# Two of the first stage's token blocks at 384 columns instead of three at 256

## The chip, the cores and the metric

The kernel runs as one program on one core of one Trainium2 chip. The number that is compared is the device time of one execution in microseconds (us), the median of several. A core has five engines that run their own instruction streams and wait for each other by semaphores: TensorE (PE, matrix products; its weight loads are shown as PEld), VectorE (DVE), ScalarE (ACT), GpSimd (POOL) and SyncE (SP), which here issues the DMAs.

## The reference

q, k and v are [4, 8, 576, 64]: batch, heads, positions, features. All arithmetic is float32.

```python
# attention: two parts, added
q_d, k_d, v_d = (mean over groups of 4 positions)          # 144 positions
out_up = repeat(softmax(q_d k_d^T / 8) v_d, 4 times)       # coarse part
out_local = softmax(where(|i-j| < 4, q k^T / 8, -1e9)) v   # a window of 7 positions
x = (out_up + out_local) as [2304 tokens, 512]
# first stage (called stage 1 here), d_ff = 1536
xn = x / rms(x) * rms_g
g = xn @ w_gate
x = (g * sigmoid(g) * (xn @ w_val)) @ w_out
# second stage (stage 2), d_ff = 2048
x = relu(x @ w_in)**2 @ w_out2
```

## The kernel before

**Numbers.** A float32 product is made of three passes in the faster fp32r format: every operand is split into a high and a low part (tiles `hi`/`lo`, `xh`/`xl`, `hh`/`hl`), and TensorE does high x high, high x low and low x high. The weights come in 64-bit words from DRAM and are split by `decode`: one ACT operation, four or five on VectorE, and an addition, a rounding and a subtraction that go to GpSimd, ACT or VectorE.

**Attention.** The first batch is done by TensorE (`wide`, `wide_post`, six pieces of 96 tokens). The coarse part of all batches is done in 16 pieces (`down`, a batch and a pair of heads each). The local part of the other three batches is done on GpSimd and VectorE in 14 units of mostly 128 tokens (`attend`, `local`): for each of a unit's four rows GpSimd multiplies queries with a window of keys (`pr<-k,q`), VectorE sums (`sc<-pr`), and later GpSimd multiplies the window of values with the weights (`pr<-v,es`) and VectorE sums into `xa`. There are two `xa` buffers (`XAB`). `post` adds the coarse part, computes the root mean square with a small TensorE product (`t<-ss,on`), scales, transposes and writes a block's input tiles `xh` and `xl`. There are two of each, so the tiles of a block take the place of those of the block but one before.

**Stage 1.** The 2304 tokens are nine blocks of 256 (`BLK`). For each block six rounds `fp` go over 256 inner features each: `hidden` does 24 matmuls of the gate into PSUM bank g, tanh on ACT, a VectorE operation (`th<-th,g`), 24 matmuls of the value into bank v, a VectorE product (`v<-v,th`), a rounding (`hh<-v`, ACT or VectorE) and a subtraction (`hl<-v,hh`); `outp` then does 24 matmuls into the block's output sums, in the two banks a (even blocks) or b (odd). A matmul has a 128x128 weight and 256 columns of tokens. `y_out` copies the sums through a tile `vv` to DRAM. All 18 weight tiles of the stage stay in SBUF; those of stage 2 take their places while the last block runs.

**Stage 2.** Four blocks of 512 tokens and one of 256, 16 rounds each of 128 inner features.

**Order.** `PLAN` is a string that sets the order in which work is recorded: d coarse pieces, a and b the first batch, w weights, u units, p posts, x the rounds of stage 1 (`SEQ` gives the order of the first twelve, which belong to two blocks). Buffers are handed out in that order, in rings, so a tile waits for the user of the same buffer that was recorded before it. `Plan.order` then sorts the operations with a model of their times, forward and backward in turn, `ROUNDS` times with a random jitter (`SEED`), and keeps the best. The instructions are issued in that order on every engine; what may run on more than one engine (`VP`, `AV`) is assigned there. `TAGS` names the PSUM banks of the coarse pieces and the first batch, and for each half of a weight tile how it is decoded. Until stage 1 begins, idle time of TensorE is filled with dummy matmuls (line 466, into bank v).

Of the kernel before, what the change touches and what calls it, by code (L numbers as in the profile page):

```python
# [13 lines left out]
F32 = mybir.dt.float32  # L14
# [34 lines left out]
TAGS = ('dbg- dtg- dbg- dgg- bdd- bdd- bdd- bdd- ttd- ttd- ttd- ttd- add- add- add- add- '  # L49
        'aagg aagg aagt bbtd bbdd bbtd bdt tdt gta gdt gdt btt '  # L50
        '-- -- a3 a3 -- -- -- -- -- -- -- -- -- -- -- -- -- -- -- g1 g1 -- -- -- -- -- -- -- -- -- -- -- -- -- -- --')
# [12 lines left out]
SEED = 1  # L64
# [412 lines left out]
def attn_moe_kernel(ctx: ExitStack, tc, qs, kw, vw, qt, kt, vt, v4, wg, wv, wo, w2i, w2o, gw, gb,  # L477
# [7 lines left out]
    seq1 += [(j, fp) for j in range(len(set(SEQ)), len(BLK)) for fp in range(NP1)]  # L485
# [13 lines left out]
    def bank(tag, dtype=F32):  # L499
        return tile("ps", tag, [128, 512], dtype, 2 if tag in "ab" else 1)  # L500
# [5 lines left out]
    g_sb = tile("const", "g", [128, 4])  # L506
    mk_sb = tile("const", "mk", [128, 70])
    xr_sb = tile("const", "xr", [128, 4, 64])
# [34 lines left out]
    def decode(src, n, hi, lo, st, how="--"):  # L543
# [6 lines left out]
        low = lw if how[0] == "-" else bank(how[0], I32)  # L550
        A.activation(low, lw.bitcast(U32), AF.Copy, scale=2.0**-29)
        part = lw if how[1] == "1" else low
        V.scalar_tensor_tensor(out=part, in0=hw, scalar=-0x40000000, in1=low, op0=ALU.bitwise_and,
# [10 lines left out]
        if how[1] == "3":  # L564
            hf = low.bitcast(F32)
        AV.copy(hi[:, cs], hf)
        (V if how[1] == "3" else VP).tensor_tensor(out=lo[:, cs], in0=hf, in1=hi[:, cs].bitcast(F32), op=ALU.subtract)
# [27 lines left out]
    def weights1(fp, m):  # L595
        src = (wg, wv, wo)[m]
        n = fp * 3 + m
        how = TAGS.split()[28 + 2 * n:30 + 2 * n]
        hi, lo = slots(n) if n < 16 else [spare([128, 1024], F32R) for i in range(2)]
        for n in range(2):  # L600
            st = staging() if fp < 5 else tile("stage", "st", [128, 512, 2], I32, 3)
            decode(src[fp], n, hi, lo, st, how[n])
        W1[fp, m] = hi, lo
# [93 lines left out]
    def xtile(j):  # L697
        if j not in xtiles:
            xtiles[j] = [tile("xt", t, [128, 4, BN], F32R, 2) for t in ("xh", "xl")]
        return xtiles[j]  # L700
# [155 lines left out]
    def post(j):  # L856

        xh, xl = xtile(j)
        n0 = 0
        if j == 2:  # L860
            n0 = 64
            AV.copy(xh[:, :, 0:64], xr_sb)
            VP.tensor_tensor(out=xl[:, :, 0:64], in0=xr_sb, in1=xh[:, :, 0:64].bitcast(F32), op=ALU.subtract)
        nt = (BN - n0) // RUNS
        ss = tile("sm", "ss", [128, 8], F32, 2)
        mb = bank("t")
        o = 0
        for u in BLOCKS[j]:
            w = u.cnt
            od = tile("lc", "pr", [128, 2, 128], F32, 2)[:, 0:w // 2]  # L870
            a = 0
            for s in u.segs:
                DQ.dma_start(
                    out=od[:, a:a + s.cnt // 2],
                    in_=od_d[s.b - 1].rearrange("(p u) e -> p u e", u=NU)[:, s.t // 2:(s.t + s.cnt) // 2])
                a += s.cnt // 2
            xv = u.xa.rearrange("p (a w) e -> p a w e", w=2)
            VP.tensor_tensor(out=xv, in0=xv, in1=od.unsqueeze(2).to_broadcast([128, w // 2, 2, 128]), op=ALU.add)
            for i in range(w):
                A.activation(mb[:, 0:128], u.xa[:, i, :], AF.Square, accum_out=ss[:, o + i:o + i + 1])  # L880
            o += w
        mp = mb[:, 128:128 + nt]
        T.matmul(out=mp, lhsT=on_sb, rhs=ss[:, 0:nt], start=True, stop=True)
        ms = tile("sm", "ms", [128, 8], F32, 2)[:, 0:nt]
        V.tensor_scalar(out=ms, in0=mp, scalar1=1.0 / DM, scalar2=1e-6, op0=ALU.mult, op1=ALU.add)
        P.tensor_tensor(out=ms, in0=ms, in1=half_neg[:, 0:nt], op=ALU.pow)
        o = 0
        for u in BLOCKS[j]:
            w = u.cnt
            for i in range(w):  # L890
                A.activation(u.xa[:, i, :], u.xa[:, i, :], AF.Copy, scale=ms[:, o + i:o + i + 1])
            tp = bank("t")
            with plan.joint():
                for i in range(w):
                    T.transpose(tp[:, i * 128:(i + 1) * 128], u.xa[:, i, :], id_sb)
            tv = tp[:, 0:w * 128].rearrange("p (x k c) -> p k x c", k=4, c=RUNS)
            ns = slice(n0 + o * RUNS, n0 + (o + w) * RUNS)
            for k in range(4):
                hv, lv = (t[:, k, ns].rearrange("p (x c) -> p x c", c=RUNS) for t in (xh, xl))
                g = g_sb[:, k:k + 1]  # L900
                A.activation(hv, tv[:, k], AF.Copy, scale=g)
                V.scalar_tensor_tensor(out=lv, in0=tv[:, k], scalar=g, in1=hv.bitcast(F32), op0=ALU.mult,
                                       op1=ALU.subtract)
            o += w

    yps, hid = {}, {}

    def gemm(p, w, xh, xl, c):
        whi, wlo = (t.rearrange("p (k f) -> p k f", k=4) for t in w)
        cs = slice(c * 128, c * 128 + 128)  # L910
        with plan.joint():
            for k in range(4):
                T.matmul(out=p, lhsT=whi[:, k, cs], rhs=xh[:, k, :], start=(c == 0 and k == 0), stop=False,
                         skip_group_check=True)
                T.matmul(out=p, lhsT=whi[:, k, cs], rhs=xl[:, k, :], start=False, stop=False,
                         skip_group_check=True)
# [3 lines left out]
    def hidden(j, fp):  # L920
        xh, xl = xtiles[j]
        n = BLK[j]
        gp = bank("g")[:, 0:2 * n].rearrange("p (c n) -> p c n", c=2)
        for c in range(2):
            gemm(gp[:, c, :], W1[fp, 0], xh, xl, c)
        th = tile("hp", "th", [128, 2, n], F32, 2)
        A.activation(th, gp, AF.Tanh, scale=0.5)
        V.scalar_tensor_tensor(out=th, in0=th, scalar=1.0, in1=gp, op0=ALU.add, op1=ALU.mult)
# [250 lines left out]
```

## Time and profile before

| | |
|---|---|
| median of 3 runs | 1000.95 us (1000.70 to 1002.62) |
| the profiled execution | 1000.25 us, span 998.0 us |
| granted TensorE clock, mean | 0.998 |

```profile
PE 980.2 (98%) x6866; PEld 906.4 (91%) x6866; DVE 587.6 (59%) x985; ACT 417.0 (42%) x984; POOL 442.3 (44%) x298
...
PE   7998999999999999999999999999999999999998
...
DVE  6999899786687857575634568963222322322232
...
POOL 2566688867656676676733465863001000100000
```

The first line is the busy time of each engine with its share of the span and its instructions. The others cut the span into 40 slices of 25 us; a digit is the busy share of a slice in tenths. TensorE is busy nearly all the time after the first slices, VectorE is full in the first quarter and GpSimd has most of its work in the first half.

### The profile page before, as it was taken

Reading aid. Unit: us, or ns where it says so; the run is one execution under the profiler, and the core shown is the slowest. Engines: PE = TensorE matmul, PEld = TensorE weight load, DVE = VectorE, ACT = ScalarE, POOL = GpSimd, SP = SyncE. Lnnn points to the kernel's source line nnn. Section 1 sums busy time; section 2 is a strip of 40 time slices with the busy share of each in tenths; the row PEclk is TensorE's granted clock in tenths of the full one; section 3 lists DMA queues with packets and bytes.
Section 4 is the critical chain, followed back from the end, with each engine's and each line's share of the span. In section 5 each row is a group of like instructions: output and inputs, shape, how many; then the busy total and the mean of one; then the engine's idle time right before and its main releaser. Section 6 shows DMA issues by size and latency. Waiting matters only on the chain.

```text
span 998.0 us, 17246 instructions
## 1 busy us (share of the span) xinstructions
PE 980.2 (98%) x6866; PEld 906.4 (91%) x6866; DVE 587.6 (59%) x985; ACT 417.0 (42%) x984; POOL 442.3 (44%) x298
## 2 busy tenths in 40 slices
PE   7998999999999999999999999999999999999998
PEld 7888999999999999999999998888888888888897
DVE  6999899786687857575634568963222322322232
ACT  5787665532435342323244557663222212322232
POOL 2566688867656676676733465863001000100000
PEclk9999999999999999999999999999999999999999
DMA  9954553253262523222011446334000100100010
GB/s 282 262 160 157 175 179 103 73 151 113 85 182 80 171 78 115 93 65 96 28 33 60 132 128 209 104 109 137 1 1 1 54 0 1 43 1 1 1 43 22
DMA packets 38465, 92.93 MB, mean 93 GB/s; under 512 B 4218, under 2 KB 14498, under 8 KB 38386
## 3 DMA queue, kind: packets, MB, share of 16 engines
q1 hardware_dynamic: 38386, 91.84, 29.6%
q8 instruction: 54, 0.88, 0.4%
q14 instruction: 25, 0.20, 0.1%
HBM read 80.62 MB, written 11.21 MB: 92 GB/s over the span
## 4 chain that ended last, share of the span: by engine, by line
PE 89%; DVE 5%; POOL 2%; DMA 2%; issue 1%; ACT 1%; SPq 0%; DVEq 0%; POOLq 0%; ACTq 0%
PE v L473 25%; PE g L473 24%; PE a L473 20%; PE b L473 15%; DVE b L473 2%; PE d L473 2%; DVE st L473 2%; PE t L473 2%; PE v L466 1%; DMA b<-in_qt 1%; DMA st<-in_wg 1%; POOL w L473 0%; POOL st L473 0%; POOL pr L473 0%; POOL b L473 0%
## 5 line engine op out<-in xcount | busy, mean ns | idle before, releaser
L473 PE MATMUL g<-xh,w 128*128 128x256 f32 (+1 forms) x776 | 176.8, 307 | 0.4 <-DVE th L473 0.4
L473 PE MATMUL v<-xh,w 128*128 128x256 f32 (+1 forms) x632 | 147.6, 311 | 0.5 <-DVE hl L473 0.5
L473 DVE SCALAR_TENSOR_TENSOR v<-v,th 128x512 f32<-128x512 f32 (+1 forms) x94 | 63.3, 674 | 128.6 <-ACT th L473 101.3
L473 PEld LDWEIGHTS g<-xh,w 128*128 128x128 f32 x776 | 131.1, 191 | 7.0 <-ACT xh L473 0.6
L473 ACT ACTIVATE th<-g 128x512 f32<-128x512 f32 (+1 forms) x94 | 54.5, 580 | 198.1 <-PE g L473 194.8
L473 POOL TENSOR_TENSOR pr<-v,es 128x896 f32<-128x896 f32 x54 | 99.4, 1939 | 65.7 <-DVE es L473 28.2
L473 PE MATMUL v<-xh,b 128*128 128x256 f32 (+1 forms) x552 | 123.9, 303 | 0.1
L473 POOL TENSOR_TENSOR pr<-k,q 128x896 f32<-128x896 f32 x54 | 115.4, 2158 | 9.6 <-DVE sc L473 7.2
L473 PE MATMUL g<-xl,w 128*128 128x256 f32 (+1 forms) x388 | 118.3, 305 | 0.1
L473 PEld LDWEIGHTS v<-xh,w 128*128 128x128 f32 x632 | 107.7, 191 | 7.1 <-PE g L473 0.7
L473 POOL TENSOR_TENSOR xl<-st,xh 128x1024 fp32r<-128x1024 f32 (+1 forms) x10 | 21.6, 2179 | 184.7 <-ACT xh L473 184.7
L473 PE MATMUL v<-xl,w 128*128 128x256 f32 (+1 forms) x316 | 97.9, 310 | 0.0
L473 PEld LDWEIGHTS v<-xh,b 128*128 128x128 f32 x552 | 93.0, 191 | 4.4 <-PE g L473 0.3
L473 PE MATMUL g<-xh,b 128*128 128x256 f32 (+1 forms) x408 | 94.4, 310 | 0.2 <-DVE th L473 0.2
L473 ACT CAST hh<-v 128x512 fp32r<-128x512 f32 (+1 forms) x94 | 53.5, 569 | 81.6 <-DVE v L473 71.3
L473 PE MATMUL v<-xl,b 128*128 128x256 f32 (+1 forms) x276 | 83.1, 301 | 0.0
L473 DVE SCALAR_TENSOR_TENSOR g<-g,th 128x512 f32<-128x512 f32 (+1 forms) x40 | 25.8, 645 | 95.5 <-ACT th L473 95.4
L473 DVE TENSOR_TENSOR hl<-v,hh 128x512 fp32r<-128x512 f32 (+1 forms) x94 | 62.4, 664 | 26.3 <-ACT hh L473 24.6
L473 PEld LDWEIGHTS g<-xl,w 128*128 128x128 f32 x388 | 74.1, 191 | 3.6 <-DVE xl L473 0.3
L473 POOL TENSOR_TENSOR st<-st 128x512 int32<-128x512 int32 x48 | 55.9, 1166 | 41.5 <-DVE st L473 39.4
L473 PEld LDWEIGHTS g<-xh,b 128*128 128x128 f32 x408 | 69.1, 190 | 4.2 <-issue 0.3
L473 ACT ACTIVATE st<-st 128x512 int32<-128x512 uint32 (+1 forms) x96 | 64.7, 684 | 18.7 <-DVE st L473 11.2
(207 smaller groups left out, 2336.8 us busy)
## 6 DMA issues: line engine op xcount, KB each, us to landing
k<-in_kw SPq DMA_DIRECT2D x12, 640.0 KB
v<-in_vw SPq DMA_DIRECT2D x12, 640.0 KB
st<-in_w2i SPq DMA_DIRECT2D x14, 512.0 KB
st<-in_w2o SPq DMA_DIRECT2D x14, 512.0 KB
y<-vv SPq DMA_DIRECT2D x18, 256.0 KB
out<-xh SPq DMA_DIRECT2D x18, 256.0 KB
st<-y SPq DMA_DIRECT2D x8, 512.0 KB
st<-in_wg SPq DMA_DIRECT2D x7, 512.0 KB
```

Source lines behind the costliest of these rows:

```text
L466: self.nc.tensor.matmul(out=out, lhsT=one, rhs=one, start=True, stop=True)
L473: getattr(self.hw[on[op]], method)(*args, **kw)
```

## The change

- `BLK` becomes six blocks of 256 and two of 384 tokens. The units of the last three blocks are spread over two: the seventh block takes three units, the eighth three.
- In a block of 384, `hidden` does its work in pieces of 128 inner features: 12 matmuls of 384 columns into g, 12 into v, the same four operations on 128x384 instead of 128x512, and `outp` 12 matmuls. The output sums take four banks (a, a, b, b). `outp` records its work in four groups, one for each output slice, and a slice that is complete is copied out at once.
- `post` works on one unit instead of a block: each unit has its own small product for the root mean square, its own scale and its own transposes.
- `th` has one buffer instead of two, in stage 2 too; `vv` is gone, and `y_out` uses the ring `st` that the weights and the later coarse pieces are staged in (for the last block a tile of the ring `xh`). Its copy may go to ACT or VectorE.
- The special ways to decode four halves of weight tiles are gone: two halves (`a3`) had their additions and subtraction on VectorE with the low part in PSUM bank a, two (`g1`) held the low part in bank g. All halves are now decoded in SBUF.
- `PLAN`, `SLOT`, `TAGS`, `ROUNDS` and `SEED` are others.

```diff
-         5: [[(2, 4, 4)], [(2, 8, 4)]], 6: [[(2, 12, 4)], [(2, 16, 2), (3, 16, 2)]],
-         7: [[(3, 0, 4)], [(3, 4, 4)]], 8: [[(3, 8, 4)], [(3, 12, 4)]]}
-BLK = [256] * 9
+         5: [[(2, 4, 4)], [(2, 8, 4)]], 6: [[(2, 12, 4)], [(2, 16, 2), (3, 16, 2)], [(3, 0, 4)]],
+         7: [[(3, 4, 4)], [(3, 8, 4)], [(3, 12, 4)]]}
+BLK = [256, 256, 256, 256, 256, 256, 384, 384]
...
-PLAN = 'd2 d3 d0 d1 a0 b0 w00 a2 a1 w01 w12 b1 a4 b2 a3 a5 w11 w21 b4 w20 w10 b3 w02 w30 u1 w32 b5 d7 u0 d5 d4 d6 w22 E w31 w41 w40 w50 x x w42 x x d10 x x w52 w51 x x x x x p2 x u2 d11 u3 p3 x d8 x x u5 d9 u4 x x x p4 u6 x x d12 x x x d15 d14 d13 x u7 p5 u8 x u9 x x x x x p6 x x x u10 x x x u11 x x p7 x x u12 u13 x x x x x x x x p8 x x x x x x'
-SLOT = [7, 8, 9, 1, 0, 4, 5, 2, 6, 3, 0, 1, 3, 4, 5, 2]
-ROUNDS = 38
+PLAN = 'd2 d3 d0 d1 a0 b0 w00 a2 a1 w01 w12 b1 a4 b2 a3 w02 a5 w11 w21 b4 w32 w10 b3 w30 u1 w20 b5 d7 u0 d5 d4 d6 w22 E x w41 w40 w50 w42 d10 w31 x x w51 x x x x x w52 x x x p0 p1 x d8 u2 d11 u3 p2 p3 x d9 x x u5 u4 x x x p4 p5 u6 d14 d13 x x x x x x d15 u7 p6 p7 u8 x u9 d12 x x x x x x p8 p9 x x x u10 x x p10 u11 x p11 x x u12 u13 x p12 p13 x x x x x x x x'
+SLOT = [7, 8, 5, 3, 0, 4, 9, 2, 6, 1, 5, 0, 4, 3, 2, 1]
+ROUNDS = 37
...
-SEED = 1
+SEED = 3
...
-        low = lw if how[0] == "-" else bank(how[0], I32)
-        A.activation(low, lw.bitcast(U32), AF.Copy, scale=2.0**-29)
+        A.activation(lw, lw.bitcast(U32), AF.Copy, scale=2.0**-29)
...
-        if how[1] in "-1":
-            VP.tensor_tensor(out=hw, in0=hw, in1=part, op=ALU.add)
-        else:
-            V.tensor_tensor(out=low if how[1] == "3" else hw, in0=hw, in1=low, op=ALU.add)
...
+        VP.tensor_tensor(out=hw, in0=hw, in1=lw, op=ALU.add)
         AV.copy(hi[:, cs], hf)
...
-    def post(j):
+    def post(u):
...
+        w = u.cnt
+        ss = tile("sm", "ss", [128, 4], F32, 2)[:, 0:w]
         mb = bank("t")
...
+        mp = mb[:, 128:128 + w]
+        T.matmul(out=mp, lhsT=on_sb, rhs=ss, start=True, stop=True)
...
     def hidden(j, fp):
+
         xh, xl = xtiles[j]
         n = BLK[j]
...
+        for cs in ((0, 1),) if n <= 256 else ((0,), (1,)):
+            w = len(cs)
+            gp = bank("g")[:, 0:w * n].rearrange("p (c n) -> p c n", c=w)
+            for i, c in enumerate(cs):
+                gemm(gp[:, i, :], W1[fp, 0], xh, xl, c, i == 0)
+            th = tile("hp", "th", [128, w, n])
+            A.activation(th, gp, AF.Tanh, scale=0.5)
+            V.scalar_tensor_tensor(out=th, in0=th, scalar=1.0, in1=gp, op0=ALU.add, op1=ALU.mult)
+            vp = bank("v")[:, 0:w * n].rearrange("p (c n) -> p c n", c=w)
...
+            yield [(j, 2 * fp + c, hh[:, i, :], hl[:, i, :]) for i, c in enumerate(cs)]
+
+    def y_out(j, m):
+        n, n0 = BLK[j], start[j]
+        w = 512 // n
+        if j == len(BLK) - 1:
+            if m == 0:
+                yps[j, "out"] = tile("xt", "xh", [128, 4, n], F32, 2)
+            ys = yps[j, "out"][:, m:m + w]
+        else:
+            ys = tile("stage", "st", [128, w, n], F32, 3)
+        AV.copy(ys, yps[j][m // w])
...
+    def outp(parts):
+
+        j, f0 = parts[0][:2]
+        w = 512 // BLK[j]
+        if f0 == 0:
+            yps[j] = [bank(b)[:, 0:w * BLK[j]].rearrange("p (m n) -> p m n", m=w)
+                      for b in ("aabb" if w == 1 else "ab"[j % 2] * 2)]
+        for m in range(4):
...
+            if sp and m % w == w - 1:
+                y_out(j, m - w + 1)
...
-        r = tile("hp", "th", [128, n], F32, 2)
+        r = tile("hp", "th", [128, n])
```

## Rows read from the trace of the kernel before

**Rows 1.** Stretch, its us, busy PE, PEld, DVE, ACT, POOL (instructions), clock, DMA share, GB/s.

```profile
0.00:95.30 95.30, 84.00 (x764) 76.43 (x765) 82.66 (x158) 68.87 (x213) 49.98 (x46) 0.98 0.70 216
95.30:200.00 104.70, 102.58 (x881) 101.52 (x881) 93.06 (x141) 61.83 (x130) 81.25 (x60) 1.00 0.45 134
200.00:430.00 230.00, 229.68 (x1982) 229.08 (x1981) 163.25 (x299) 86.10 (x256) 149.71 (x89) 1.00 0.38 116
...
530.00:603.50 73.50, 73.40 (x601) 72.74 (x600) 42.38 (x66) 38.30 (x63) 37.32 (x29) 1.00 0.39 125
...
950.00:998.00 48.00, 44.08 (x277) 39.51 (x275) 14.07 (x32) 12.46 (x32) 0.00 (x0) 0.99 0.09 34
```

**Rows 2.** The same for the dummy matmuls alone (line 466; PE and PEld).

```profile
0.00:95.30 95.30, 40.94 (x302) 37.69 (x302) 0.98 0.70 216
```

**Rows 3.** The chain that ended last, merged pieces: start, length, engine, what.

```profile
462.86 2.88 PE a L473 x24
...
600.67 2.87 PE a L473 x24
...
613.55 2.72 PE v L473 x12
```

**Rows 4.** TensorE in order of time around a small product of `post`: start, length.

```profile
362.10 0.28 PE L473 MATMUL t<-ss,on 128*128 128x8 f32 x2
362.24 0.36 PE L473 MATMUL v<-xh,b 128*128 128x256 f32 x1
362.44 0.28 PE L473 MATMUL v<-xl,b 128*128 128x256 f32 x1
```

**Rows 5.** TensorE in order of time, one round of a block of 256.

```profile
504.09 0.28 PE L473 MATMUL g<-xh,w 128*128 128x256 f32 x1
...
505.53 0.28 PE L473 MATMUL v<-xh,w 128*128 128x256 f32 x1
...
506.97 0.28 PE L473 MATMUL b<-hh,w 128*128 128x256 f32 x1
```

**Rows 6.** VectorE in order of time behind that round.

```profile
506.36 0.69 DVE L473 SCALAR_TENSOR_TENSOR th<-th,g 128x512 f32<-128x512 f32 x1 [2.05 <-ACT th L473]
507.17 0.70 DVE L473 SCALAR_TENSOR_TENSOR v<-v,th 128x512 f32<-128x512 f32 x1
508.57 0.69 DVE L473 TENSOR_TENSOR hl<-v,hh 128x512 fp32r<-128x512 f32 x1 [0.71 <-ACT hh L473]
```

**Rows 7.** VectorE's groups by shape, 0 to 100 us: count, busy us, mean ns.

```profile
L473 DVE TENSOR_TENSOR xl<-t,xh 128x384 fp32r<-128x384 f32 x4 | 2.2, 545 | 0.0
...
L473 DVE TENSOR_TENSOR w<-a,w 128x512 fp32r<-128x512 f32 x2 | 1.3, 674 | 0.0
...
L473 DVE SCALAR_TENSOR_TENSOR a<-st,a 128x512 int32<-128x512 int32 x1 | 0.7, 680 | 0.0
L473 DVE CUSTOM_DVE_ANT_0 a<-st,a 128x1024 uint16<-128x1024 uint16 x1 | 0.7, 680 | 0.0
```

**Rows 8.** Groups by shape, whole span: the decode's usual forms.

```profile
L473 POOL TENSOR_TENSOR st<-st 128x512 int32<-128x512 int32 x48 | 55.9, 1166 | 41.5 <-DVE st L473 39.4 <-POOL st L473 1.3 <-DVE b L473 0.4
L473 DVE SCALAR_TENSOR_TENSOR st<-st 128x512 int32<-128x512 int32 x47 | 44.4, 947 | 3.3 <-ACT st L473 3.0
L473 POOL TENSOR_TENSOR w<-st,w 128x512 fp32r<-128x512 f32 x29 | 40.5, 1397 | 19.7 <-ACT w L473 19.5
```

**Rows 9.** GpSimd in order of time: value products of the eleventh and the last unit.

```profile
426.25 7.29 POOL L473 TENSOR_TENSOR pr<-v,es 128x896 f32<-128x896 f32 x4 [6.38 <-ACT xh L473]
...
495.73 7.46 POOL L473 TENSOR_TENSOR pr<-v,es 128x896 f32<-128x896 f32 x4 [3.33 <-DVE es L473]
```

**Rows 10.** VectorE: last input writes of units eleven, twelve and the last.

```profile
477.30 0.61 DVE L473 SCALAR_TENSOR_TENSOR xl<-t,g,xh 128x128 fp32r<-128x128 f32 x2 [0.44 <-ACT xh L473]
...
483.56 0.87 DVE L473 SCALAR_TENSOR_TENSOR xl<-t,g,xh 128x128 fp32r<-128x128 f32 x3
...
529.11 0.87 DVE L473 SCALAR_TENSOR_TENSOR xl<-t,g,xh 128x128 fp32r<-128x128 f32 x3 [0.44 <-ACT xh L473]
```

More of the change, by code (lines that the diff above doesn't have):

```diff
@@ L541, in attn_moe_kernel, with decode @@
     late = []
-    def decode(src, n, hi, lo, st, how="--"):
+    def decode(src, n, hi, lo, st):
         DQ.dma_start(out=st.rearrange("p n w -> p (n w)"),
@@ L601, in weights1 @@
             st = staging() if fp < 5 else tile("stage", "st", [128, 512, 2], I32, 3)
-            decode(src[fp], n, hi, lo, st, how[n])
+            decode(src[fp], n, hi, lo, st)
         W1[fp, m] = hi, lo
@@ L882, in post @@
[L882 to L904, printed above, removed]
@@ new lines, in post @@
+        for i in range(w):
+            A.activation(mb[:, 0:128], u.xa[:, i, :], AF.Square, accum_out=ss[:, i:i + 1])
+        mp = mb[:, 128:128 + w]
+        T.matmul(out=mp, lhsT=on_sb, rhs=ss, start=True, stop=True)
+        ms = tile("sm", "ms", [128, 4], F32, 2)[:, 0:w]
+        V.tensor_scalar(out=ms, in0=mp, scalar1=1.0 / DM, scalar2=1e-6, op0=ALU.mult, op1=ALU.add)
+        P.tensor_tensor(out=ms, in0=ms, in1=half_neg[:, 0:w], op=ALU.pow)
+        for i in range(w):
+            A.activation(u.xa[:, i, :], u.xa[:, i, :], AF.Copy, scale=ms[:, i:i + 1])
@@ new lines, in post @@
+        tp = bank("t")
+        with plan.joint():
+            for i in range(w):
+                T.transpose(tp[:, i * 128:(i + 1) * 128], u.xa[:, i, :], id_sb)
+        tv = tp[:, 0:w * 128].rearrange("p (x k c) -> p k x c", k=4, c=RUNS)
+        ns = slice(u.col, u.col + w * RUNS)
+        for k in range(4):
+            hv, lv = (t[:, k, ns].rearrange("p (x c) -> p x c", c=RUNS) for t in (xh, xl))
+            g = g_sb[:, k:k + 1]
+            A.activation(hv, tv[:, k], AF.Copy, scale=g)
+            V.scalar_tensor_tensor(out=lv, in0=tv[:, k], scalar=g, in1=hv.bitcast(F32), op0=ALU.mult,
+                                   op1=ALU.subtract)
@@ L922, in hidden @@
         n = BLK[j]
[L923 to L928, printed above, removed]
-        vp = bank("v")[:, 0:2 * n].rearrange("p (c n) -> p c n", c=2)
-        for c in range(2):
-            gemm(vp[:, c, :], W1[fp, 1], xh, xl, c)
@@ L932, in hidden @@
-        V.scalar_tensor_tensor(out=vp, in0=vp, scalar=0.5, in1=th, op0=ALU.mult, op1=ALU.mult)
-        hh = tile("hp", "hh", [128, 2, n], F32R, 2)
-        hl = tile("hp", "hl", [128, 2, n], F32R, 2)
-        hid[j, fp] = (hh, hl)
-        AV.copy(hh, vp)
-        V.tensor_tensor(out=hl, in0=vp, in1=hh.bitcast(F32), op=ALU.subtract)
-    def y_out(j):
-        n, n0 = BLK[j], start[j] % 512
-        for m2 in range(2):
-            ys = tile("hp", "vv", [128, 2, n], F32, 2)
-            A.copy(ys, yps[j][m2])
-            DQ.dma_start(out=y_d[start[j] // 512][:, 2 * m2:2 * m2 + 2, n0:n0 + n], in_=ys)
@@ new lines, in outp @@
+    def outp(parts):
[5 more added lines that the diff above has]
+        for m in range(4):
+            o = yps[j][m // w][:, m % w, :]
+            mc = slice(m * 128, m * 128 + 128)
+            with plan.joint():
+                for _, f, hh, hl in parts:
+                    whi, wlo = (t.rearrange("p (c m) -> p c m", c=2)[:, f % 2, mc] for t in W1[f // 2, 2])
+                    st, sp = f == 0 and m % w == 0, f == 2 * NP1 - 1
+                    T.matmul(out=o, lhsT=whi, rhs=hh, start=st, stop=False, skip_group_check=True)
+                    T.matmul(out=o, lhsT=whi, rhs=hl, start=False, stop=False, skip_group_check=True)
+                    T.matmul(out=o, lhsT=wlo, rhs=hh, start=False, stop=sp, skip_group_check=True)
+            if sp and m % w == w - 1:
+                y_out(j, m - w + 1)
@@ L976, in attn_moe_kernel @@
             u.cnt = sum(s[2] for s in segs)
+            u.col = BLK[j] - RUNS * sum(s[2] for segs in blk for s in segs) + RUNS * sum(o.cnt for o in BLOCKS[j])
             for s in segs:
@@ L1018, in attn_moe_kernel @@
         elif c[0] == "p":
-            post(n)
+            post(units[n])
         elif c[0] == "w":
```

108 lines of the change are left out of this document (43 added, 65 removed).

## The prediction

> **What bounds the kernel now.** I read the busy times by stretch first. They have TensorE idle for 11.3 us before 95.3 us, for 2.1 us from there to 200, for 0.3 to 430, 0.1 between 530 and 603.5 and 3.9 at the end [rows 1]. That is all of the 17.8 us between its 980.2 busy us and the span, so from about 95 us to 950 the time is TensorE's own work, one instruction behind the other, at full clock. Next I read the dummy matmuls: 40.9 us of the busy time before 95.3 are theirs [rows 2]. So in that first stretch only some 43 us of TensorE are real work; it waits for the attention of the first batch and for weights to be decoded. VectorE is busy 82.7 of 95.3 us there and 93.1 of the next 104.7 [rows 1], and is what limits this stretch. The first matmul of stage 1 runs at 95.3 us, and whatever moves that point moves the end by as much, as long as TensorE finds work behind it. Last I read the chain for the price of a matmul, since from 95 us on the chain is nearly all TensorE: 24 matmuls of 256 columns take 2.88 us, 12 of 512 columns 2.72 us, and stage 1 ends at 600.67 + 2.87 = 603.5 us [rows 3].
>
> **The wider matmuls.** 2.88/24 is 120.0 ns for 256 columns, 2.72/12 is 226.7 ns for 512 [rows 3]. The difference, 106.7 ns for 256 columns, is one column in a cycle of 2.4 GHz; what is left at either width is 13.3 ns for each matmul, whatever its width. No matmul here has 384 columns. On the line through both, one takes 160.0 + 13.3 = 173.3 ns. The last 768 tokens now need three blocks of six rounds of 72 matmuls, 1296 at 120.0 ns, 155.5 us. After the change they need two blocks of six rounds of 72, 864 at 173.3 ns, 149.8 us. That is 432 matmuls fewer at 13.3 ns, 5.8 us gained, all of it in the stretch in which TensorE has no idle time. The bounds: if the time grew in proportion to the columns up to 384 (120.0 x 1.5 = 180.0 ns), nothing is gained; if it stood on 512's rate (226.7 x 0.75 = 170.0 ns), 8.6 us are. I take the line, since the same 13.3 ns shows at both ends of it.
>
> The Trainium skill, "TensorE: Matmul & The Clock Gate", section "Back-to-back issue gap", gives N/2.4 + 2.5 ns for a warm matmul, 109 ns at 256 columns. The trace has 120.0 and decides. By the page 432 matmuls fewer would be worth only 1.1 us, and the sum below would come out at about 1001.4 us.
>
> **The small products of `post`.** Seven blocks had one each, 14 units have one each: seven more. One holds TensorE for 0.14 us, and the first matmul behind it takes 0.20 us to the next start where 0.12 is usual, so 0.22 us [rows 4], seven times 1.5 us. The bounds are 0.14 and 0.28 us each, 1.0 and 2.0. The transposes are as many as before. Six more VectorE or GpSimd operations on four columns lie where VectorE is busy 163 of 230 us [rows 1] and cost nothing; without that cover they would be under 2 us, off TensorE.
>
> **Half rounds on one g and one v bank.** In the trace, g's second half starts at 504.09 and ends at 505.53, v follows until 506.97, then 2.88 us of output sums, then the next g of 1.44 and only then v again [rows 5]: bank g has 1.44 + 2.88 = 4.3 us until it is written again, and v 2.88 + 1.44 = 4.3 us. The operations that free v run from 507.17 to 508.57 + 0.69 = 509.26, done 2.3 us after v's end; those that free g end at 507.05, 1.5 us after g's end [rows 6]. In the block of 384 a group of 12 takes 12 x 173.3 ns = 2.08 us and either bank has two groups, 4.16 us, almost what it has now. The operations are shorter: 545 ns for 384 columns [rows 7] for 690 now. So no wait is added; 1.9 us of cover is left for a VectorE operation that comes between. A single `th` buffer asks that the v product of a piece be done before the next tanh, 2 groups later, and it is; in stage 2 a round is 24 matmuls of 227 ns, 5.4 us, and hides it more easily. The four sum banks must be copied within the next piece's g and v, 4.16 us, for four copies of about half a microsecond. I cost all this at nothing; were the cover short by 0.35 us in each of block seven's 12 pieces, the gain would be gone.
>
> **The decode.** Without `a3`, VectorE loses two additions of 0.68 and two subtractions of 0.67 us, 2.7 us, in the stretch it limits [rows 7]; GpSimd gets two of 1.17 and two of 1.40, up to 5.1 us [rows 8], of which it has 45 idle us before 95.3 [rows 1]. The combining operation takes 680 ns with one operand in PSUM [rows 7] and 947 with all in SBUF [rows 8]: four halves, 1.1 us more on VectorE. At best VectorE's 2.7 us and the 2.1 us of TensorE's later idle time both go, -4.8. At worst GpSimd's 5.1 us stand on the way of the first weights and the 1.1 comes on top, +6.2. The new order string, banks, slots and seed sort this stretch afresh; the trace does not show how, and I keep them in the same bounds. I take nothing, between the two.
>
> **The queues.** `y_out` in the ring `st` stands before later coarse pieces in record order: their loads on SP wait until block 0's outputs have left, and with them TensorE's and VectorE's part of those pieces. They work towards units of later blocks and hold nothing that stage 1 needs at once, so I take nothing; if they make a unit late, that is priced with the first rival.
>
> **Sum.** 1000.25 (the profiled execution; span 998.0 and 2.25 around it) - 5.8 + 1.5 = 996.0. That execution lies 0.7 us under the median of the runs, 1000.95. So I predict a median of 996.7 us.
>
> **What is late next.** A block of 384 needs three units. Stage 1 would end at 603.5 - 4.2 = 599.3, its last block start 12 x 6.24 = 74.9 us earlier, at 524.4, and the one before at 449.5. The eleventh unit is due at 449.5; in the trace its input is finished at 477.30 + 0.61 = 477.9 [rows 10]. But there it belongs to the next block and waits for its partner: its value products end at 426.25 + 7.29 = 433.5, after 6.4 us of waiting for a buffer of a unit that waited for its own partner [rows 9]. From the last unit's products, 503.2 [rows 9], to its last input, 530.0 [rows 10], a `post` of a block takes 26.8 us; I estimate half, 13.4, for a unit alone, half the operations. Then the eleventh is ready at 446.9, or at 440.5 without the wait: in time by 3 to 9 us. The last unit would be ready at 516.6, due 524.4.
>
> **Rivals.**
> - *The eleventh unit is late.* If a unit's `post` keeps the 26.8 us and the wait stays, its input comes at 460.3, TensorE stands 10.8 us before block seven, and the time is 1007.5. For it: the margin is small and GpSimd does 150 of 230 us in the stretch before [rows 1], so units can't come much closer. Against: 80 us of GpSimd's time there are idle. It turns the result when the input is more than 4.2 us late. 0.12 for slower by this and by all else.
> - *The start gives the gain back, or the line fails at 384.* The first stretch ends 2.5 to 6 us later, 999.2 to 1002.7; or a 384 column matmul takes 180 ns and the small products are all that is left, 1002.5. For it: VectorE has little room. Against: what is taken from VectorE is about what it is given back. 0.14. The change then does not do what it says on the clock.
> - *The start gets shorter too.* VectorE's 2.7 us and the 2.1 go: 991.9. 0.08.
> - The forecast, 996.7, with 3 us to either side for the first stretch: 0.66.
>
> Slower or faster than 0.2% (2 us) is what a measurement of this kernel can tell from no change. The forecast and the shorter start are faster (0.74), the second rival is within 0.2% (0.14), a late unit slower (0.12). The range goes from the shorter start, 992, to the second rival's end, 1002.5; outside are the late unit and little else.
>
> **What would show it.** Right: TensorE's 12 matmuls of 384 columns in 2.08 us; no idle time of it between 200 and 950; 14 small products; the first matmul of stage 1 within 3 us of 95.3; stage 1 ending near 599. Wrong: 12 in 2.16 us; a gap before the seventh block's first g or between its pieces; a first matmul some microseconds later, or more than 2.1 us idle between it and 200.

## The result, and the profile after

The changed kernel takes 1006.17 us in the median of five runs (1003.85 to 1009.21), the kernel before 1000.95 beside it: 1.0051 of before, interval 1.0027 to 1.0075. Run once more beside other kernels it took 1004.80 us and stood at 1.0021 (1.0006 to 1.0036). It is slower by 2 to 5 us where 4.3 faster were forecast. The profiled execution took 1003.85 us, its span is 1001.8, 3.8 more than the span before.

The stretches of [rows 1], in the trace after:

```profile
0.00:95.30 95.30, 77.88 (x701) 69.11 (x702) 86.05 (x154) 67.55 (x210) 52.88 (x49) 0.96 0.71 214
95.30:200.00 104.70, 95.46 (x794) 94.52 (x794) 90.47 (x139) 59.71 (x124) 78.49 (x57) 0.93 0.44 131
200.00:430.00 230.00, 229.59 (x1983) 229.08 (x1983) 164.49 (x303) 85.77 (x254) 157.66 (x97) 1.00 0.36 112
430.00:530.00 100.00, 99.66 (x639) 99.14 (x638) 58.82 (x110) 34.14 (x106) 57.11 (x33) 1.00 0.17 51
530.00:603.50 73.50, 73.50 (x423) 73.05 (x422) 48.78 (x79) 39.82 (x71) 36.44 (x28) 1.00 0.40 133
```

Between 200 and 603.5 us TensorE is idle for less than 1 us, as before. Between 95.3 and 200 it is idle for 9.2 us, where it was 2.1, and the granted clock is 0.93 for 1.00. Its dummies (line 465 now), 302 and 40.9 us in [rows 2], are fewer:

```profile
0.00:95.30 95.30, 28.63 (x216) 26.53 (x216) 0.96 0.71 214
```

The chain of waits, pieces that answer to [rows 3] (start, length, what); the second and third are the first piece of a block of 384:

```profile
112.06 5.46 PE g L472 x24
...
450.99 2.08 PE g L472 x12
453.08 2.08 PE v L472 x12
```

Twelve matmuls of 384 columns take 2.08 us, 173.3 ns each, as forecast. But 24 of 256 at 112 us take 5.46 us, where 2.88 is the price at full clock; from there to 200 us TensorE never waits.

How far stage 1 has come shows best in a count. These are TensorE's groups of 256 columns up to 120 us (the number behind x is the count), first before, then after:

```profile
L473 PE MATMUL g<-xh,w 128*128 128x256 f32 x48 | 9.6, 288 | 0.4 <-DVE th L473 0.4
L473 PE MATMUL v<-xh,w 128*128 128x256 f32 x40 | 8.2, 292 | 0.0
L473 PE MATMUL g<-xl,w 128*128 128x256 f32 x24 | 6.9, 287 | 0.1
L473 PE MATMUL v<-xl,w 128*128 128x256 f32 x20 | 5.7, 283 | 0.0
L473 PE MATMUL a<-hh,w 128*128 128x256 f32 x15 | 2.8, 283 | 0.0
L473 PE MATMUL a<-hl,w 128*128 128x256 f32 x8 | 2.3, 283 | 0.0
```

```profile
L472 PE MATMUL g<-xh,w 128*128 128x256 f32 x32 | 9.9, 394 | 4.5 <-DVE b L472 3.6 <-DVE th L472 0.9
L472 PE MATMUL v<-xh,w 128*128 128x256 f32 x29 | 6.3, 296 | 0.0
L472 PE MATMUL g<-xl,w 128*128 128x256 f32 x16 | 6.1, 383 | 0.0
L472 PE MATMUL v<-xl,w 128*128 128x256 f32 x14 | 4.2, 298 | 0.3 <-DVE xl L472 0.3
```

155 matmuls of stage 1 were done by then before, 91 after, and none of the output sums (`a<-hh`, `a<-hl`). Up to 200 us the same count gives 767 and 703: the 64 stay missing. At 120.0 ns [rows 3] they are 7.7 us. With the forecast's own 5.8 and 1.5 that closes the account of the spans: 998.0 - 5.8 + 1.5 + 7.7 and 0.4 more idle time between 200 and 530 is 1001.8. The change won what was forecast in its wide blocks, and lost more in the first stretch. I call this number **the count by 120 us** below.

TensorE's waits in the trace after, 90 to 113 us (start, length, what, in brackets the idle time and what ended it):

```profile
94.20 0.58 PE L472 MATMUL g<-xh,w 128*128 128x256 f32 x1 [3.60 <-DVE b L472]
...
107.77 0.90 PE L472 MATMUL t<-id,b 96*128 96x96 f32 x4 [6.19 <-DVE b L472]
110.47 0.67 PE L472 MATMUL d<-id,pe 96*72 96x96 f32 x3 [1.80 <-DVE pt L472]
112.06 0.55 PE L472 MATMUL g<-xh,w 128*128 128x256 f32 x1 [0.93 <-DVE th L472]
```

All are waits for VectorE. What VectorE does in front of the longest, and GpSimd in the same time:

```profile
102.37 4.68 DVE L472 SCALAR_TENSOR_TENSOR st<-st 128x512 int32<-128x512 int32 x1 [0.59 <-ACT st L472]
106.97 0.74 DVE L472 SCALAR_TENSOR_TENSOR b<-t,b,b 96x512 f32<-96x512 f32 x1
```

```profile
101.97 1.29 POOL L472 TENSOR_TENSOR b<-b,b 128x512 fp32r<-128x512 f32 x1
103.22 1.04 POOL L472 TENSOR_TENSOR b<-b 128x512 int32<-128x512 int32 x1
104.22 1.04 POOL L472 TENSOR_TENSOR st<-st 128x512 int32<-128x512 int32 x1
105.22 1.29 POOL L472 TENSOR_TENSOR w<-b,w 128x512 fp32r<-128x512 f32 x1
```

The combining operation of a decode, 0.68 us at its shortest, lasts 4.68: it ends 0.54 us behind the end of the last of four GpSimd operations that follow each other without a gap. The operation that TensorE waits for stands behind it.

### The profile page after: what moved, and what is told of

Its sections match the earlier page's. It is cut to its first block, busy times and chain, and to the rows that moved or that the text cites. A ratio compares the mean times of both kernels' runs of the same rounds, so it can differ in the third digit from the quotient of the medians.

```text
span 1001.8 us, 16331 instructions
## 1 busy us (share of the span) xinstructions
PE 970.6 (97%) x6362; PEld 895.3 (89%) x6362; DVE 599.9 (60%) x1006; ACT 419.2 (42%) x998; POOL 449.8 (45%) x309
## 4 chain that ended last, share of the span: by engine, by line
PE 88%; DVE 5%; DMA 3%; POOL 1%; issue 1%; ACT 1%; SPq 0%; DVEq 0%; POOLq 0%; ACTq 0%
PE g L472 25%; PE v L472 25%; PE a L472 19%; PE b L472 17%; DVE st L472 2%; PE d L472 2%; DMA w<-in_v 2%; DVE b L472 1%; PE t L472 1%; POOL w L472 1%; DMA st<-in_wg 0%; DMA st<-in_wo 0%; DMA st<-in_wv 0%; POOL b L472 0%; DVE vs L472 0%
## 5 line engine op out<-in xcount | busy, mean ns | idle before, releaser
L472 PE MATMUL g<-xh,w 128*128 128x256 f32 (+2 forms) x712 | 177.1, 323 | 4.6 <-DVE b L472 3.6
L472 PE MATMUL v<-xh,w 128*128 128x256 f32 (+2 forms) x584 | 145.6, 322 | 0.0
L472 DVE SCALAR_TENSOR_TENSOR v<-v,th 128x512 f32<-128x512 f32 (+2 forms) x100 | 64.4, 644 | 135.2 <-ACT th L472 97.4
L472 PE MATMUL v<-xh,b 128*128 128x256 f32 (+2 forms) x504 | 121.0, 314 | 0.3 <-DVE ms L472 0.3
L472 PE MATMUL g<-xl,w 128*128 128x256 f32 (+2 forms) x356 | 114.2, 321 | 0.0
L472 PE MATMUL v<-xl,w 128*128 128x256 f32 (+2 forms) x292 | 93.8, 321 | 0.3 <-DVE xl L472 0.3
L472 PE MATMUL g<-xh,b 128*128 128x256 f32 (+2 forms) x376 | 92.7, 320 | 0.0
L472 DVE TENSOR_TENSOR hl<-v,hh 128x512 fp32r<-128x512 f32 (+2 forms) x100 | 63.3, 633 | 31.4 <-ACT hh L472 30.9
L472 PE MATMUL v<-xl,b 128*128 128x256 f32 (+2 forms) x252 | 78.8, 313 | 0.0
L472 DVE TENSOR_SCALAR st<-st 128x512 f32<-128x512 f32 (+1 forms) x98 | 70.9, 724 | 11.8 <-ACT st L472 11.2
```

Of the source, the lines that this page charges most:

```text
L472: getattr(self.hw[on[op]], method)(*args, **kw)
```

## The experiments

Theory 1: the wide blocks give what was forecast and the new order of the first stretch takes more away. Theory 2: something in the wide blocks, the single banks or the outputs' ring costs it. All ratios are to the kernel before, run beside each kernel on the same chip. An order written into a kernel is one that is read from a table instead of searched.

**The old start (e1_old_start).** The changed kernel with before's decodes, bank letters, slots, `post` by block for blocks two to five, and before's order up to about 170 us. To keep that order its sums in blocks of 256 are one group of 24 again.

```
-SLOT = [7, 8, 5, 3, 0, 4, 9, 2, 6, 1, 5, 0, 4, 3, 2, 1]
+SLOT = [7, 8, 9, 1, 0, 4, 5, 2, 6, 3, 0, 1, 3, 4, 5, 2]
-PLAN = '... a3 w02 a5 w11 w21 b4 w32 w10 b3 w30 u1 w20 ...'
+PLAN = '... a3 a5 w11 w21 b4 w20 w10 b3 w02 w30 u1 w32 ... r2 x u2 ...'
-        first = {op: op.n for op in self.ops}
+        first = {op: int(n) for op, n in zip(self.ops, rank)}
```

> The blocks of 384 tokens, the single g and v banks, the single tanh buffer and the outputs through the ring st stay as in the changed kernel. The first stretch is put back: decodes through banks a and g, bank letters, slots, posts by block for blocks two to five, and up to about 170 us the order of work of the kernel before, written into the kernel instead of searched. Theory 1 (the wide blocks give what was forecast, the re-sorted first stretch takes it away): the profiled execution of before, 1000.25, less 5.8 for the matmuls, plus 0.7 for three more small products, is 995.1, so a median of 995 to 998 and a first stretch like before's: TensorE idle some 2 us between 95 and 200 us, first matmul of stage 1 near 95 us. Theory 2 (something in the wide blocks, the single banks or the outputs' ring costs it): with the old start still 1001 or more, and idle time of TensorE behind 200 us.

Measured: 0.9951 (0.9936 to 0.9965), 998.37 us. Count 156. The stretch of the loss:

```profile
95.30:200.00 104.70, 101.64 (x872) 100.31 (x871) 93.09 (x142) 62.57 (x130) 79.79 (x59) 1.00 0.43 132
```

Idle 3.1 us and full clock. The median lies 0.4 us above the 995 to 998 that theory 1 gave, and well under theory 2's 1001: the same wide blocks, banks, tanh buffer and ring gain 4.9 us with this start, by the medians. The spans of the two profiled executions, 998.0 and 996.0, differ by 2.0 only: e1 is idle for 0.9 us more between 95.3 and 200 and for 2.5 us between 200 and 530, where before is for 0.3. So theory 2 is not wholly empty, but it does not make the loss.

**Is it the clock? (e3_dummies_on, e4_gate_first.)** The dummies' end and the cold clock are the most striking thing in the trace after. The first run lets them go on into a bank of block 0's sums, the second puts the first value products behind their gate products.

```
+                    more = more and (self.idle2, True) not in op.uses
-                    if fill and free:
+                    if more and free:
```

```
+        i = order.index(gate) + 1
+        order[i:i] = [(gate[0] + times[gate[1]], op) for _, op in value]
```

> The changed kernel with its plan and order untouched; only the dummy matmuls go on longer. They write to bank v and end when stage 1's first value product takes that bank, at 75 us. Here they go on into a bank for block 0's sums, until those are first written (about 122 us), wherever TensorE would wait. If the fall of the granted clock (0.50 in 90 to 95 and 105 to 115 us) is what costs, TensorE's matmuls there run at 120 ns for 227 and the time falls by 3 to 6 us, to 1000 to 1003. If what TensorE waits for (VectorE's and the decodes' order) is what costs, the clock is full but the waits only grow longer by what the matmuls save: less than 1.5 us, 1004.7 or more.

> The changed kernel with one item moved in TensorE's order: the first round's value matmuls (two groups of 12) stand behind its gate matmuls, as they stand in every later round, so the dummies go on until about 94 us. If the dummies' end at 75 us and the cold clock behind it are the loss: 2 to 5 us faster than the changed kernel, 1001 to 1004. If the order of VectorE's work and the weights' decodes is the loss, within 1.5 us of it, since the value matmuls done early only filled idle time; slower by up to 3 if they come to stand on the path.

Measured: 1.0031 (1.0018 to 1.0043) and 1.0014 (0.9999 to 1.0029), counts 78 and 80, against 1.0021 and 1.0051 for the changed kernel. TensorE in the trace after, and then in that of e3 (busy, clock in the middle):

```profile
95.00:105.00 10.00, 6.25 (x50) 0.84 0.53 153
105.00:115.00 10.00, 4.51 (x21) 0.50 0.55 167
```

```profile
95.00:105.00 10.00, 9.25 (x86) 1.00 0.56 179
105.00:115.00 10.00, 6.73 (x48) 0.83 0.45 130
```

The clock came back, to 1.00 and 0.83, and the time did not. But e3 does not clear the clock, since its dummies came to stand on the chain of waits itself, before and between the products that they were to warm (line 467 is the dummies):

```profile
110.25 2.51 PE a L467 x12
...
113.01 1.37 PE a L467 x12
114.38 1.44 PE g L474 x12
115.81 1.11 PE a L467 x10
116.92 1.43 PE g L474 x12
118.35 1.11 PE a L467 x10
```

The gate products take 2.87 us for 5.46, and the dummies between and behind them take 2.2 of the 2.6 us back. In e4 the same 24 products still run at the low clock, 5.46 us from 113.61. It shows that the early end of the dummies is not the loss: 1005.34 us is not in the 1001 to 1004 that the clock's theory gave, and is within 1.5 us of the changed kernel. The products that ran cold in front of 112 us have a wait for VectorE behind them and lose nothing by it, but behind those at 112 us no wait follows: up to 2.6 of the 7.7 us may be the clock's, and no run parts that off.

**The decodes (e5_plain_decode).** The kernel before with its four decodes through banks `a` and `g` made ordinary, planner's number 14.

```
-        '-- -- a3 a3 -- ... -- g1 g1 -- ...')
+        '-- -- -- -- -- ... -- -- -- -- ...')
```

> The kernel before with one of the change's edits alone: the four decodes that put their parts into banks a and g are ordinary ones, as in the changed kernel; the order is searched anew from another seed (the best of 24 by the kernel's own planner). If giving up these decodes is what hurts the start, 1003 to 1008, with the first value product some 15 us earlier, the dummies ending there, and idle time of TensorE of 6 us or more between 95 and 200 us. If they are worth nothing, 999.5 to 1002.

Measured: 0.9982 (0.9963 to 1.0001), count 144. The dummies end early here too (220 of them), the clock between 95.3 and 120 us is 0.72, and the time is no longer. In this order giving up these decodes costs nothing that shows: what the prediction's decode part weighed was not the matter.

**GpSimd's holds (a0_changed_again, e6_guards).** Five operations of VectorE stand long in the trace after. Behind each, GpSimd gets a tiny operation that reads its result; no engine's order is changed.

```
+GUARD = (96, 108, 133, 147, 165)
+                        if nv - 1 in GUARD:
+                            one = kw["out"][:, 0:1].bitcast(I32)
+                            self.nc.gpsimd.tensor_tensor(out=gd[0:one.shape[0]], in0=one, in1=one, op=ALU.add)
```

> The changed kernel once more, unaltered, beside the runs below on one chip. Every theory: 0.3 to 0.8% over the kernel before.

> The changed kernel with its plan and its order on every engine untouched. Five VectorE operations of its first 110 us stood while GpSimd went from one operation into the next (54.68 us: 2.66 us for 0.11; 63.42: 3.51 for 0.68; 79.81: 3.65 for 0.68; 89.51: 3.09 for 0.35; 102.37: 4.68 for 0.68), 15.1 us of standing, of which about 10 lies behind the end of the first GpSimd operation. Behind each of the five GpSimd gets one tiny added operation (one column) that reads what the VectorE operation writes, so that it lets VectorE in after one operation instead of two to four. Theory 1a (GpSimd holding VectorE up is what this start loses): those five take 0.7 to 2.2 us each, TensorE's waits for VectorE between 90 and 112 us shrink by half or more, and the time falls by 3 to 7 us, to 999 to 1003. Theory 1b (the holds are cover only; the order of decodes and weights is what is late): within 1.5 us of the changed kernel, or slower by up to 2, since GpSimd now waits.

Measured: 1.0021 (1.0006 to 1.0036) unaltered, less than the 0.3% expected at least, and 0.9999 (0.9987 to 1.0012) with the guards, 2.4 us between the medians (1004.80 and 1002.38). The operation at 102.37 us, the guard on GpSimd (`gd`), and TensorE's wait behind:

```profile
103.16 1.53 DVE L474 SCALAR_TENSOR_TENSOR st<-st 128x512 int32<-128x512 int32 x1 [0.47 <-POOL b L474]
```

```profile
103.11 1.03 POOL L474 TENSOR_TENSOR b<-b 128x512 int32<-128x512 int32 x1
104.77 0.19 POOL L479 TENSOR_TENSOR gd<-st 128x1 int32<-128x1 int32 x1 [0.63 <-DVE st L474]
104.91 1.04 POOL L474 TENSOR_TENSOR st<-st 128x512 int32<-128x512 int32 x1
```

```profile
105.41 0.90 PE L474 MATMUL t<-id,b 96*128 96x96 f32 x4 [2.92 <-DVE b L474]
```

1.53 us for 4.68, and a wait of 2.92 us for 6.19. Of the others, 2.66, 3.65 and 3.09 us became 0.96, 1.24 and 0.59, though an operation two places behind the last now stands 1.50 us for 0.42; the one at 63.42 us still took 2.49 and missed its forecast. TensorE's waits for VectorE between 90 and 113 us fall from 12.9 to 9.2 us, not by the half that was expected. The holds are real and are a part, 2 to 3 us; the count is 100, still 55 short. The gain lies a little under the 3 us that I expected at least.

**Only this draw? (s16_other_seed, s4_other_seed, b15_old_other_seed.)** Every edit makes the planner search again, and its random part gives another order for another number.

```
-SEED = 3
+SEED = 16
```

> The changed kernel with another number for the random part of its planner (16 for 3): the same instructions in another order. Theory 1 (the edits cost nothing in the start; this one order of it does): another order lies elsewhere, by some microseconds, and the less VectorE is held up before 125 us the better: 996 to 1003. Theory 2 (the edits make any start worse, for instance by the single tanh buffer): 1004 or more here too.

> The same with the number 4. Theory 1: differs from both other orders by some microseconds, to either side, 998 to 1012, in the order of VectorE's time held up by GpSimd before 125 us. Theory 2: within 2 us of the changed kernel.

> The kernel before, nothing but the number of its planner's random part changed (15 for 1): the same instructions in another order. If the order that the kernel before had was a good one among many (the changed kernel lost by having to take another): 2 to 8 us slower than before, with fewer than the 155 matmuls of stage 1 that it had done by 120 us. If its edits make its start good in any order: within 1.5 us of before.

Measured: the changed kernel with 16: 0.9980 (0.9965 to 0.9994), with 4: 1.0053 (1.0032 to 1.0075); the kernel before with 15: 0.9973 (0.9954 to 0.9993). So the draw alone moves the time by 7 us, but before's own order was no lucky one: another is better still. And the counts, 72 and 48 for the changed kernel, 163 for the one before, do not mix. VectorE's held time did not rank them either (4 is the slowest with less of it than 16), so holds are not the whole cause. The profiled execution of 16 was its slowest run (1005.99, median 1000.68), so its count stands for a bad execution.

**A third start (e9_third_start).** e5's start with the wide blocks, order written in as in e1.

> The changed kernel's blocks of 384 with a third start: that of the run e5 (the four decodes ordinary, as in the changed kernel; posts by block for blocks two to five; e5's order up to about 170 us, written into the kernel). e5 stood at 0.9982 of before with nine blocks of 256. If start and wide blocks are worth what they are apart, this is 0.9982 less the 0.5% that the wide blocks gave on the old start: 0.992 to 0.995 of before. If the wide blocks gain only with the old start: 0.997 or more.

Measured: 0.9966 (0.9947 to 0.9985), count 111. From e5's 0.9982 that is a gain of 1.6 us, less than the 3 to 6 expected, with intervals that overlap. Its runs spread from 997.37 to 1003.64 us, and the profiled one is the slowest: VectorE has the same sequence as in e5's trace there, and is 3.8 us behind it by 90 us; between 200 and 530 us TensorE is idle for 4.4 us, in e5 for 1.7.

**The record string (b_new_record_order, a_old_record_order).** The new string, slots and letters put into the kernel before; the old string and slots put into the changed one.

```
-PLAN = 'd2 ... a3 a5 w11 w21 b4 w20 w10 b3 w02 w30 u1 w32 ...'
+PLAN = 'd2 ... a3 w02 a5 w11 w21 b4 w32 w10 b3 w30 u1 w20 ...'
```

> The kernel before (nine blocks of 256, two tanh buffers, posts by block, outputs' own tiles) with only what the change did to its start: the new string of record order, the new weight slots, the new bank letters, ordinary decodes; another planner number (23). Seen so far: with the old string the kernels had done 144 to 163 matmuls of stage 1 by 120 us (one execution 111), with the new string 48 to 100, whatever the planner's number. Theory A (the new string and slots make the start late): 100 or fewer by 120 us, and 1.003 to 1.008 of before. Theory B (only the planner's draw does, strings are alike): 110 or more and 0.995 to 1.002.

> The changed kernel with only its record string (as far as stage 1's sixth block) and its weight slots put back; bank letters, ordinary decodes, posts by unit, single tanh buffer, outputs' ring and blocks of 384 as in the changed kernel; another planner number (22). Theory A: 130 or more matmuls of stage 1 by 120 us and 0.993 to 0.998 of before. Theory B: anything from 0.997 to 1.006, with the count by 120 us anywhere from 50 to 150.

Measured: 0.9982 (0.9969 to 0.9995) with a count of 132, and 1.0053 (1.0034 to 1.0072) with 77. The reverse of my theory A in both: the string and the slots do not carry the loss. But the counts still part the kernels cleanly, 48 to 91 and 111 to 163 among those whose order was searched or written in. What the first have in common is the rest of the change.

**The split of the sums (f_split_sums, f_one_tanh, g_joint_sums, g_joint_first3, g_joint_first1).** One edit that the prediction passed over. The list of the change puts the four groups under the blocks of 384, but the code has them in every block: before, a round's 24 matmuls of output sums are one group that the planner places as a whole; after, they are four groups of six, one for each `m`, that it may spread. Put into the kernel before alone, beside the single tanh buffer alone:

```
-        with plan.joint():
-            for c in range(2):
-                for m in range(4):
+        for m in range(4):
+            with plan.joint():
+                for c in range(2):
```

```
-        th = tile("hp", "th", [128, 2, n], F32, 2)
+        th = tile("hp", "th", [128, 2, n])
```

and taken out of the changed kernel, in all blocks of 256, in the first three, in block 0 alone (`product` is the loop's old body). Each of the five also has a planner number, and so an order, of its own:

```
+        if j < 1:
+            with plan.joint():
+                for part in parts:
+                    for m in range(4):
+                        sp = product(m, part)
```

> The kernel before with one edit of the change alone: a round's 24 matmuls of output sums are four groups of six, which the planner may place apart, instead of one group; another planner number (2). Theory S (the split makes the start late: four groups released as soon as a round is done compete with the attention for TensorE and move the planner's order): 100 or fewer matmuls of stage 1 by 120 us, and 1.002 to 1.008 of before. If the split is harmless: 110 or more, 0.995 to 1.002.

> The kernel before with another edit alone: one tanh buffer instead of two; another planner number (5). Theory S: 115 or more matmuls of stage 1 by 120 us, 0.996 to 1.002 of before. Theory H (the single buffer makes the start late): 100 or fewer, and 1.002 to 1.008.

> The changed kernel with one edit taken out: in the blocks of 256 a round's 24 matmuls of output sums are one group again (in the blocks of 384, where each bank holds one sum, four groups as in the changed kernel); another planner number (41). Theory S: 115 or more matmuls of stage 1 by 120 us (the changed kernel 91 and 75), some 4 to 6 us won there; behind 200 us up to 4 us of it may be lost again, since TensorE has no small groups to fill gaps: 0.995 to 1.002 of before. If the split is harmless: 100 or fewer, and 1.002 or more.

> As the run before, but one group only in the first three blocks, and four groups of six from the fourth on, as in the changed kernel; another planner number (20). Theory S: 120 or more by 120 us, without the loss behind 200 us: 0.993 to 0.998 of before, near the run with the old start (0.995). If the split is harmless: 100 or fewer, and 1.002 or more.

> The changed kernel with one group of 24 for the output sums of block 0 alone; four groups of six in blocks 1 to 5; another planner number (79). If the start is late because block 0's small groups come between the attention's products: 115 or more matmuls of stage 1 by 120 us and 0.993 to 0.999 of before. If it takes the sums of blocks 1 and 2 as well: 100 or fewer and 1.001 or more.

| run | block 0's sums | blocks of 384 | count by 120 us | ratio, interval |
|---|---|---|---|---|
| f_split_sums | four groups | no | 99 | 1.0011 (0.9999 to 1.0022) |
| f_one_tanh | one | no | 124 | 1.0020 (1.0003 to 1.0036) |
| changed kernel | four | yes | 91, 75 | 1.0051, 1.0021 |
| g_joint_sums | one | yes | 154 | 0.9969 (0.9951 to 0.9986) |
| g_joint_first3 | one | yes | 163 | 0.9964 (0.9948 to 0.9981) |
| g_joint_first1 | one | yes | 136 | 0.9947 (0.9931 to 0.9963) |

The counts come out as the split says in all five. A draw moves a count too, so I set all orders that the planner searched side by side. With four groups in block 0 they have 91 (75 in a second execution), 72, 48, 77 and 99; with one group 155, 163, 144, 132, 124, 154, 163 and 136. Over thirteen orders the two do not overlap, though in none could the split be changed and the order kept.

Neither the low clock nor idle time is needed for a low count. In f_split_sums the clock is full, TensorE is idle for 1.6 us in this stretch, and the first matmul of stage 1 comes at 104.7 us, behind 356 dummies for 302:

```profile
95.30:200.00 104.70, 103.14 (x893) 102.28 (x892) 92.73 (x145) 59.52 (x124) 79.42 (x61) 1.00 0.47 144
```

With block 0's sums alone in one group, the last run's groups up to 120 us:

```profile
L472 PE MATMUL g<-xh,w 128*128 128x256 f32 x43 | 12.7, 374 | 1.8 <-DVE b L472 1.0 <-DVE th L472 0.8
L472 PE MATMUL g<-xl,w 128*128 128x256 f32 x21 | 7.5, 358 | 0.0
L472 PE MATMUL v<-xh,w 128*128 128x256 f32 x32 | 6.5, 288 | 0.4 <-DVE hl L472 0.4
L472 PE MATMUL v<-xl,w 128*128 128x256 f32 x16 | 4.6, 289 | 0.7 <-DVE xl L472 0.7
L472 PE MATMUL a<-hh,w 128*128 128x256 f32 x16 | 3.0, 283 | 0.0
L472 PE MATMUL a<-hl,w 128*128 128x256 f32 x8 | 2.3, 283 | 0.0
```

The sums are back, as one piece of 24 in the chain at 112.64 us; in the trace after the first six come at 122.41. This is the changed kernel with one edit taken back in one block, and another draw: 998.05 us, 0.9947, the lowest ratio of all with e1's 0.9951. Among the kernels with blocks of 384, those with four groups in block 0 and an order of their own stand at 0.9980 to 1.0053, the five with one group (e1 and e9 too) at 0.9947 to 0.9969. Among the kernels with blocks of 256 alone the times do not part: 1.0011 with the split, 0.9973 to 1.0020 without. There the split missed its forecast of 1.002 or more, and the tanh buffer alone lies at the end of its range; a single edit's price is within what a draw moves.

**A hold in another order (g_joint3_guard).** g_joint_first3 with one guard, at an operation that stood 3.26 us at 83.89.

```
+GUARD = (143,)
```

> The run with one group in the first three blocks, its order untouched, with one tiny GpSimd operation behind the VectorE operation that stood 3.26 us (0.27 without a hold) at 83.89 us while GpSimd went through three operations. In front of TensorE's wait of 3.44 us for VectorE at 87.86. If holds cost here as they did in the changed kernel's order: the operation takes 0.7 to 1 us, that wait shrinks by some 2 us, and the time falls by 0.5 to 2 us, 0.995 to 0.996 of before. If not: within 0.5 us, 0.996 to 0.997.

Measured: 0.9956 (0.9939 to 0.9974) against 0.9964 without. The hold is gone, and TensorE's wait behind it is 0.78 us for 3.44, but the two medians differ by 0.2 us on two chips and the count is 145 for 163: no gain that shows, where 0.5 to 2 us were forecast.

## Why the prediction was wrong

- *The wider matmuls*: right to the digit, 2.08 us for twelve. With a like start the wide blocks gain 4.9 us (e1 to before, by the medians; 2.0 by the profiled spans) or 1.6 (e9 to e5), where 5.1 were due with the products that these kernels have.
- *The small products*: 14, as said (28 records, two for each). Half rounds on one bank, the queues, the late unit: in the changed kernel, with less than 1 us idle between 200 and 603.5 us, none of them shows. Other orders do show them: one wait of 1.02 to 1.30 us for VectorE inside the seventh block (g_joint_sums, s16, e9), and 0.66 us for the last block's input (e1, g_joint_first1). "I cost all this at nothing" was right for this order, and not for every one.
- *The first stretch* is the step that failed: "The new order string, banks, slots and seed sort this stretch afresh; the trace does not show how, and I keep them in the same bounds. I take nothing". By the count it was +7.7 us in the profiled execution (9.6 in the second one), beyond its own upper bound of 6.2; stage 1 ended at 607.5 us, not near 599. The bounds came from the decodes, which are worth nothing that shows (e5). The edit that moves the stretch stands in the diff, though not in the lines of it shown above, and the prediction has no line on it: the `joint` around the output sums went inside the loop over `m`. With that taken back in block 0 alone, and a new draw, the time falls from 1.0021 or 1.0051 of before to 0.9947. The rival nearest to what came, a start 2.5 to 6 us later (0.14), had the place right, the size too small, and another cause.
- *The marker was wrong too.* "The first matmul of stage 1 runs at 95.3 us, and whatever moves that point moves the end by as much": it came at 75.3 us, 20 us earlier, and the end came later, since it only filled idle time. The count by 120 us is the better marker: over the kernels with blocks of 384 the profiled span falls from 1009.3 us at 48 to 993.6 at 163. It is a rough one: f_split_sums, 56 short of before, has a span 3.9 us longer, not 6.7.
- What would show it wrong was named rightly: more than 2.1 us idle between 95 and 200.

How the loss comes about within the stretch: VectorE is what TensorE waits for, and in the changed kernel it is held up more. Worked out from all its rows up to 110 us (each row's time less the shortest of its shape in any of the traces), VectorE stands 22 us before, 35 after and 28 with the guards. That is the part shown by taking it away, 2 to 3 us. It is not the whole: the three g_joint kernels stand 27 to 29 us and before with the other number 28, and their counts are 136 to 163. Why the planner, given four small groups, brings the first rounds later is argued and not shown: each can be put off by itself, so the products in front of them are due later, and the attention's and the decodes' operations come first. Nor is the loss parted between order, holds and the low clock at 112 us.

## What to carry to other kernels

Where a planner orders the work, an edit is paid for in all the work it sorts: list every change of what it may move (a group split, a buffer less), and put the uncertain stretch in the range at the size of another draw, here 7 us. Judge a start by how much work the bounding engine has done at a point from which it hardly waits, not by when it begins. Separate such a change by writing the old order into the new kernel: one run showed that gain and loss had different causes. And where filling matmuls are to test the clock, look whether they stand on the chain of waits themselves.

## What the runs showed of the hardware

- An operation of VectorE can stand while GpSimd does several: 4.68 us through four of them, and 1.53 where a guard made GpSimd pause (e6). The Trainium skill, "SBUF — State Buffer", section "Who interferes with whom", says that the two share a pair of ports, that a VectorE instruction with two inputs in SBUF contends with a GpSimd instruction that reads SBUF, and that in VectorE's two-port mode whoever issues first has the pair for its whole instruction. The operation of 4.68 us has two such inputs, and the rows agree for one instruction; here GpSimd went on into three more before VectorE was done. When VectorE gets in between two of them, as at many places in these traces, no run settles.
- TensorE's granted clock was 0.50 (1.2 GHz) between 105 and 115 us, behind 10 us in which TensorE was busy for 6.25, and 24 matmuls of 256 columns took 5.46 us for 2.88. These 24 stand behind TensorE's last wait before 200 us, so up to 2.6 us of the time may be theirs; no run shows how much (the dummies of e3 brought the clock back and took 2.2 us between the same products).
- The first stretch is not the same in two executions of one program: 91 and 75 matmuls by 120 us in the changed kernel, and runs from 1000.86 to 1008.21 us; e1's five lie within 1.8 us.
